# Window attention and feed-forward in one kernel: the first layer's first three steps split by head pair, weights joined into buffers of their own, the first loads on a second queue, and another order

## The chip, the core and the metric

The kernel runs on one core of a Trainium2 chip. The core has five engines that run side by side: TensorE (PE) for matmuls, VectorE (DVE), ScalarE (ACT), GpSimd (POOL), and SyncE (SP), which here only issues DMAs. Each engine works through its own instructions in order and waits at an instruction whose inputs are not there yet. PE writes to eight banks of PSUM; everything else lives in SBUF. The metric is the device time of one launch in microseconds, lower being better.

## What is computed

Eight batches of eight heads, 512 local and 32 global tokens, head size 64. A local query sees the 32 global keys and the local keys within 32 positions; a global query sees all keys. The 4352 result rows of 512 numbers then pass through a feed-forward layer of width 2048.

```python
s_g = scale * np.matmul(q_g, k_all.transpose(0, 1, 3, 2))
out_g = np.matmul(sm(s_g), v_all)
s_ll = np.where(np.abs(pos[:, None] - pos[None, :]) <= 32, scale * np.matmul(q_l, k_l.transpose(0, 1, 3, 2)), -1e9)
a_l = sm(np.concatenate([scale * np.matmul(q_l, k_g.transpose(0, 1, 3, 2)), s_ll], axis=-1))
out_l = np.matmul(a_l, v_all)
x = np.concatenate([out_g, out_l], axis=2).transpose(0, 2, 1, 3).reshape(B * S, H * D)
h = x @ w_in
g = h - np.tanh(h)
return g @ w_out
```

The two weight matrices arrive as 64-bit floats.

## The kernel before

**Precision.** Most operands are kept as a rounded high part and a low remainder, so one product is three passes on PE: high by high, low by high, high by low. The first two batches of attention ("plain", `Pair`) work on unsplit 32-bit data, two heads at a time; from the third batch on (`Head`) operands are split. Of the feed-forward layer, an engine other than PE makes each split: a cast (ACT or DVE) and a subtraction (mostly POOL).

**Weights.** There are 64 pieces of 128x256, in the order `w_in`, `w_in`, `w_out`, `w_out` for each of 16 hidden tiles f. For each piece `add_weights` issues a load into one of three buffers `wraw` (L364), then ACT rescales the upper words (L375), DVE shifts the lower ones (L379) and joins both in place (L383), ACT casts the high part (helper at L308) and POOL subtracts (L389). The buffer is free for the next load when the last of these has read it.

**Feed-forward layer.** A `Chunk` is the 512 local tokens of one batch, in 16 steps; a last chunk holds the 256 global tokens. A step's hidden part (L1090) is 12 matmuls of 128x512 into one bank: three passes over the four quarters of the 512 inputs. Then come tanh on ACT (L1098), the difference on DVE (L1101), the cast `ghi` and the remainder `glo` (L1107 on POOL). The step's output part (L1138) is 12 matmuls that add into four banks. x of a batch is complete when its last head pair's product (L602 in plain batches) has been cast into `x_hi` and `x_lo`.

**Overlap.** While batch b is in the feed-forward layer, the attention of batch b+1 runs between its steps. For a split head i: scores with the global queries (L779, L780), local scores (L831, L832) which read keys `kw` and queries `hi`/`hl` that DMAs have rearranged, softmax on DVE, ACT, DVE and POOL, then the product of head i-1 (L1008) which also carries the transposes of head i (L1010). So the last product of a batch waits for the scores of the next batch's first head, and a batch's feed-forward chunk cannot begin before it. I call the stretch where one chunk ends and the next begins a batch boundary; five of them (the ends of chunks 1 to 5, counted from 0) are followed by attention of a further batch.

**What sets the order.** Nothing is ordered by hand: every operation is added to `Order` with estimated durations, the keys that it reads and writes, and a due number; `Order.run` then plays the program through with these estimates and always takes the operation that can start first, the smaller due number deciding near ties. The due numbers and the penalties that choose between engines come from the table `CFG`. The order so found is emitted engine by engine. All DMAs are issued by SP in that order.

```python
                    key = (s, o.due, o.seq)
                    if best is None or s < best[0] + self.TOL and (
                            s < best[0] - self.TOL or (o.due, o.seq) < (best[1], best[2])):
                        best = (s, o.due, o.seq, o, e, d, used, t0)
```

## Time and profile before

| what | value |
|---|---|
| time, median of three runs | 1061.52 us (1059.08 to 1063.37) |
| time of the profiled execution | 1059.53 us |
| its span, first to last instruction | 1057.8 us |
| mean granted TensorE clock | 0.981 |
| moved by DMA | 91.69 MB, mean 87 GB/s |
| matmul records | 5656 |

The span is what the views of the trace cover; the 1.7 us beside it lie around it. "Busy" of PE counts overlapping matmuls once, and their ends are modelled, so the start of one to the start of the next is the better measure of a matmul's price.

### The profile page before, as it was taken

The page shows a single profiled execution, that of the slowest core. Times are in us where ns is not written, and L with a number is a line of the kernel's source. Part 1 is how long each engine was busy: PE and PEld are TensorE (multiplying, and loading weights), DVE is VectorE, ACT ScalarE, POOL GpSimd, SP SyncE. Part 2 cuts the span into 40 slices and gives each one's busy share as a digit, 9 for nine tenths or more (in the row PEclk, how much of TensorE's full clock was granted, in tenths as well). Part 3 has the DMA queues.
Part 4 walks back from the last instruction along what each step waited for, and adds up shares of the span by engine and source line. Part 5 has one row for each costly group of instructions (what it writes and reads, how often), then busy time and mean ns, then how long its engine had stood idle before and what let it go on. Part 6 is the DMA issues. An engine that isn't in the chain of part 4 may idle for free.

```text
span 1057.8 us, 19135 instructions
## 1 busy us (share of the span) xinstructions
PE 1009.3 (95%) x5656; PEld 837.6 (79%) x5656; DVE 661.7 (63%) x2084; ACT 608.4 (58%) x1684; POOL 625.9 (59%) x875
## 2 busy tenths in 40 slices
PE   6779999999996999999999999999999999999997
PEld 4557777788885888878888888888887888888896
DVE  7855666667664876687766786587757776322221
ACT  6856666656655765477657766577647765310121
POOL 5645556567664776677756776577666766522221
PEclk9979999999996999999999999999999999999999
DMA  8643444633235333454335432454335431000010
GB/s 209 166 124 106 128 113 126 143 78 82 57 77 127 79 78 69 83 137 87 73 64 137 91 85 59 95 130 86 80 60 133 91 70 42 33 8 1 1 40 20
DMA packets 253639, 91.69 MB, mean 87 GB/s; under 512 B 205408, under 2 KB 238944, under 8 KB 253536
## 3 DMA queue, kind: packets, MB, share of 16 engines
q1 hardware_dynamic: 253536, 90.48, 36.3%
q8 instruction: 45, 0.74, 0.3%
q14 instruction: 58, 0.48, 0.2%
HBM read 49.27 MB, written 8.91 MB: 55 GB/s over the span
## 4 chain that ended last, share of the span: by engine, by line
PE 88%; SPq 2%; DVE 2%; DMA 2%; issue 2%; ACT 2%; POOL 1%; POOLq 0%; ACTq 0%; DVEq 0%
PE bank L1090 35%; PE bank L1138 34%; PE bank L1008 5%; PE bank L1010 4%; PE bank L831 2%; PE bank L832 2%; PE bank L922 1%; PE bank L602 1%; PE bank L581 1%; PE bank L779 1%; SPq L640 1%; DMA hl<-hl 1%; PE bank L512 1%; DMA wraw<-in_moe_w_in_dram 1%; PE bank L780 1%
## 5 line engine op out<-in xcount | busy, mean ns | idle before, releaser
L1107 POOL TENSOR_TENSOR glo<-t,ghi 128x512 fp32r<-128x512 f32 x136 | 176.0, 1295 | 183.7 <-DVE ghi L308 80.7
L1101 DVE TENSOR_TENSOR t<-bank,t 128x512 f32<-128x512 f32 x136 | 93.8, 690 | 166.0 <-ACT t L1098 164.7
L1098 ACT ACTIVATE t<-bank 128x512 f32<-128x512 f32 x136 | 81.4, 598 | 189.4 <-PE bank L1090 172.3
L1138 PE MATMUL bank<-w_out_hi,ghi 128*128 128x512 f32 x544 | 153.9, 397 | 3.6 <-ACT ghi L308 3.6
L1138 PE MATMUL bank<-w_out_lo,ghi 128*128 128x512 f32 x544 | 154.4, 398 | 0.0
L1138 PE MATMUL bank<-w_out_hi,glo 128*128 128x512 f32 x544 | 153.4, 396 | 0.4 <-POOL glo L1107 0.4
L856 POOL TENSOR_SCALAR prob<-prob,st 128x224 f32<-128x224 f32 x240 | 108.2, 464 | 61.7 <-DVE st L851 39.6
L1090 PE MATMUL bank<-x_hi,w_in_hi 128*128 128x512 f32 x512 | 141.8, 399 | 0.4 <-ACT x_hi L308 0.4
L1090 PE MATMUL bank<-x_lo,w_in_hi 128*128 128x512 f32 x512 | 142.0, 400 | 0.0
L1090 PE MATMUL bank<-x_hi,w_in_lo 128*128 128x512 f32 x512 | 140.8, 397 | 0.0
L843 ACT ACTIVATE prob<-prob,st 128x224 f32<-128x224 f32 x240 | 113.4, 474 | 22.1 <-DVE st L836 20.7
L1138 PEld LDWEIGHTS bank<-w_out_hi,ghi 128*128 128x128 f32 x544 | 100.6, 188 | 25.1 <-ACT ghi L308 4.3
L836 DVE CUSTOM_DVE_ANT_0 prob<-bank,mask 128x224 f32<-128x224 f32 x240 | 83.4, 387 | 51.2 <-PE bank L832 41.1
L1138 PEld LDWEIGHTS bank<-w_out_lo,ghi 128*128 128x128 f32 x544 | 100.0, 189 | 19.4
L1138 PEld LDWEIGHTS bank<-w_out_hi,glo 128*128 128x128 f32 x544 | 99.2, 188 | 20.5 <-POOL glo L1107 0.8
L1090 PEld LDWEIGHTS bank<-x_hi,w_in_hi 128*128 128x128 f32 x512 | 94.6, 191 | 21.7 <-issue 1.2
L1090 PEld LDWEIGHTS bank<-x_lo,w_in_hi 128*128 128x128 f32 x512 | 92.2, 190 | 17.4 <-issue 0.6
L1090 PEld LDWEIGHTS bank<-x_hi,w_in_lo 128*128 128x128 f32 x512 | 92.1, 189 | 17.5
L1010 PE MATMUL bank<-idr,prob 128*128 128x128 f32 x376 | 99.4, 283 | 4.2 <-POOL prob L856 2.6
L1008 PE MATMUL bank<-thi,vv 128*128 128x160 f32 (+2 forms) x384 | 97.8, 296 | 0.0
L1043 POOL TENSOR_TENSOR x_lo<-wraw,x_hi 64x256 fp32r<-64x256 f32 x96 | 70.7, 736 | 39.6 <-ACT x_hi L308 26.9
L1008 PE MATMUL bank<-tlo,vv 128*64 128x160 f32 (+2 forms) x384 | 90.0, 235 | 0.0
(138 smaller groups left out, 1934.2 us busy)
## 6 DMA issues: line engine op xcount, KB each, us to landing
hl<-hl SPq DMA_DIRECT2D x72, 128.0 KB, 2.3
wraw<-in_moe_w_in_dram SPq DMA_DIRECT2D x32, 256.0 KB, 2.9
wraw<-in_moe_w_out_dram SPq DMA_DIRECT2D x32, 256.0 KB, 3.1
out_dram<-wraw SPq DMA_DIRECT2D x32, 256.0 KB, 2.3
kw<-hl SPq DMA_DIRECT2D x72, 96.0 KB, 2.2
vraw<-in_v_l_dram SPq DMA_DIRECT2D x48, 128.0 KB, 2.2
rawkq<-in_k_l_dram SPq DMA_DIRECT2D x96, 64.0 KB, 2.3
rawkq<-in_q_l_dram SPq DMA_DIRECT2D x96, 64.0 KB, 2.4
```

The source lines that it names most:

```text
L831: nc.tensor.matmul(t_[:, i, :KC], part_lo()[:, q], kw2()[:, t], start=True, stop=False)
L836: nc.vector.tensor_tensor_reduce(out=self.tile(t)[:, :KC], in0=getattr(self, f"s_{pair}")[:, i, :KC], in1=tile_mask[t], scale=-0.125, scal ...
L843: nc.scalar.activation(x, x, AF.Exp, bias=self.st[:, t:t + 1], scale=-1.0, accum_out=self.st[:, 4 + t:5 + t])
L856: nc.gpsimd.tensor_scalar(x, x, self.st[:, 8 + t:9 + t], 1.0, op0=ALU.mult, op1=ALU.mult)
L1008: nc.tensor.matmul(dst, l, r, start=i == 0, stop=i == len(mm) - 1, skip_group_check=True)
L1010: nc.tensor.transpose(*turns[i // each], idn)
L1043: eng[e].tensor_sub(places()[1], view(total, [(160, 2), (1, P)]), f32(places()[0]))
L1090: nc.tensor.matmul(self.h[s][:, j * n:(j + 1) * n], w[:, cc, f * P:(f + 1) * P], self.x()[xi][:, cc, :n], start=part == 0 and cc == 0 and ...
L1098: nc.scalar.activation(tt_[q], self.h[s], AF.Tanh)
L1101: nc.vector.tensor_sub(tt_[q], self.h.pop(s), tt_[q])
L1107: eng[e].tensor_sub(gg[q][1], tt_[q], f32(gg[q][0]))
L1138: nc.tensor.matmul(self.acc[tt], g[:, j * self.n + tt * P:j * self.n + (tt + 1) * P], low_out(f) if wi else w_out_hi[:, f], start=s == 0 a ...
```

## The change

Six things change together.

1. **Steps 0 to 2 of chunk 0 are split by head pair.** Instead of three passes over all four quarters of x, there are four operations of three matmuls (L1162), one for each quarter. A quarter of x comes from one head pair, so its three matmuls can run as soon as that pair's product is there. The bank of the hidden step is held from the first of them on.
2. **Weights are joined into other buffers.** There are four `wraw` buffers instead of three (the fourth shares its place with `qgt`, which is used later), and the join writes into one of two halves of `vraw` (`whole`). The load buffer is free after the join; the cast and the subtraction read the half.
3. **First loads on ACT.** The keys and queries of the first head pair are issued by ACT.
4. **Values are loaded for both heads of a pair in one operation**, which needs both heads' products of the pair before to be done, and the two heads of a pair share one pair of instructions for the inverse sums.
5. **Fewer memsets at the start.** `vraw` and `gt` are cleared later, the three banks not at all, of `first_v` only a 32x64 corner.
6. **The planner has other estimates** (semaphore delays, durations, a term for a change between matmul shapes) and nearly all numbers of `CFG` are new, so the order changes over the whole program.

```diff
-    SEM = {"T": 0.21, "A": 0.13, "D": 0.13, "P": 0.15, "S": 0.1}
+    SEM = {"T": 0.21, "A": 0.06, "D": 0.06, "P": 0.06, "S": 0.1}
+    FAR = {"A": 0.08, "D": 0.1}
+    HELD = {"T": 0.0, "A": 0.1, "D": 0.085, "P": 0.04, "S": 0.0}
+    TURN = 0.2
...
-    qgt = cp.tile([P, H, 2, G], F32R, name="qgt")
+    wraw.append(cp.tile([P, 256, 2], F32, name="wraw3", tag="qgt"))
...
+    whole = vraw.rearrange("p a t d -> p a (t d)")
...
-               ho=15.4658, hs=5.4507, lag=23.9151, last=0.0, newb=2, o_ld=77.6741, o_pv=13.7172, o_pvp=1.1836, o_s=-26.7655,
+               d_v=18.7031, d_w=40.8472, d_wl=13.7854, d_wn=3.035, d_xg=3.3383, d_y=0.5073, gfirst=0, ho=12.6631, hs=6.1049, lag=11.2597, last=0.0,
...
         def join(e, _):
-            v, up = box["v"].bitcast(I32), box["raw"][:, :, 1].bitcast(I32)
-            nc.vector.scalar_tensor_tensor(v, up, 3, v, op0=ALU.logical_shift_left, op1=ALU.bitwise_or)
+            v, up = [box["raw"][:, :, k].bitcast(I32) for k in range(2)]
+            box["v"] = whole[:, n % 2]
+            nc.vector.scalar_tensor_tensor(box["v"].bitcast(I32), up, 3, v, op0=ALU.logical_shift_left, op1=ALU.bitwise_or)
...
+        wj = ("wj", n % 2)
-            add(("D", 0.42), join, due, r=[key], w=[key], lock=True)
-        add(either(256, "w"), high, due, r=[key], w=[("w", kind, f, j, 0)])
-        add(subtract(256, "w"), rest, due, r=[key, ("w", kind, f, j, 0)], w=[("w", kind, f, j, 1)], res=spot)
+            add(("D", 0.42), join, due, r=[key], w=[wj], lock=True)
+        add(either(256, "w"), high, due, r=[wj], w=[("w", kind, f, j, 0)])
+        add(subtract(256, "w"), rest, due, r=[wj, ("w", kind, f, j, 0)], w=[("w", kind, f, j, 1)], res=spot)
...
-                add(("S", 1.2), load(a, (k_l, q_l)[a]), self.due(self.C["o_ld"] - 8), w=[self.key[a]], xfer=1.46)
+                add(("S" if self.j else "A", 1.1), load(a, (k_l, q_l)[a]), self.due(self.C["o_ld"] - 8) if self.j else -200 + a,
+                    w=[self.key[a]], xfer=1.46)
...
+            early = name.startswith("b0") and s < EARLY
+            for cc in range(NCC if early else 0):
+                r = [k + (xi,) for k in self.xkeys if k[2] // 2 == cc for xi in range(2)]
+                r += [("w", "i", s, cc // 2, wi) for wi in range(2)]
+                at = due if cc == NCC - 1 else base(2 * cc) + CFG["o_h0"] + CFG["hp"] * s
+                add(("T", 0.69), some(cc), at, r=r, w=[hk], res=[tk] if cc == 0 else (), alloc=[(hk, "h")] if cc == 0 else ())
-            for part in range(3):
+            for part in range(0 if early else 3):
```

Where instructions now stand is shown at three places. First, on PE near the end of the first batch's attention. Before, the hidden steps 0 and 1 (L1090) stand behind the last product (L602), four matmuls to a row:

```order
L602 MATMUL bank_105<-first_t_95,first_v 64x160
L602 MATMUL bank_105<-first_t_96,first_v 64x160
L1090 MATMUL bank_103<-x_hi_99,w_in_hi 128x512 x4
L1090 MATMUL bank_101<-x_hi_99,w_in_hi 128x512 x4
L1090 MATMUL bank_103<-x_lo_100,w_in_hi 128x512 x4
L1090 MATMUL bank_101<-x_lo_100,w_in_hi 128x512 x4
L1090 MATMUL bank_103<-x_hi_99,w_in_lo 128x512 x4
L1090 MATMUL bank_101<-x_hi_99,w_in_lo 128x512 x4
L1138 MATMUL bank_108<-w_out_hi,ghi_74 128x512
```

In the changed kernel, on PE while the third and fourth head pairs are still in their softmax (L1162 hidden, L649 product, L566 and L972 transposes, L617 scores):

```order
L1162 MATMUL bank_102<-x_hi_97,w_in_lo 128x512
L649 MATMUL bank_105<-first_t_93,first_v 64x160
...
L566 MATMUL bank_104<-idr,pg 96x64
L1162 MATMUL bank_99<-x_hi_97,w_in_hi 128x512
L1162 MATMUL bank_99<-x_lo_98,w_in_hi 128x512
L1162 MATMUL bank_99<-x_hi_97,w_in_lo 128x512
L972 MATMUL bank_106<-idr,prob_80 128x128 x4
L972 MATMUL bank_103<-idr,t_71 128x128 x4
L1162 MATMUL bank_102<-x_hi_97,w_in_hi 128x512
...
L617 MATMUL bank_100<-first_kw,first_q 128x224
```

Of the 24 matmuls of steps 0 and 1, 18 now stand ahead of the last product and six behind it; step 2 has its twelve behind the first eight output matmuls.

Second, on SP at the start of the program, before (`first_raw` are keys and queries of a pair, `first_v` its values):

```order
L420 DMA wraw_69<-in_q_g_dram 32x8x64
L364 DMA wraw_67<-in_moe_w_in_dram 128x2x256
L463 DMA first_raw<-in_k_l_dram 128x4x64 x2
L463 DMA first_raw<-in_q_l_dram 128x4x64 x2
L364 DMA wraw_68<-in_moe_w_in_dram 128x2x256
L364 DMA wraw_69<-in_moe_w_out_dram 128x512
L958 DMA first_v<-in_v_l_dram 128x3x64
```

In the changed kernel the same place on SP; the first pair's keys and queries are ACT's first four DMAs, and the `first_raw` rows here are the second pair's:

```order
L433 DMA wraw_69<-in_q_g_dram 32x8x64
L375 DMA wraw_78<-in_moe_w_in_dram 128x2x256
L375 DMA wraw_67<-in_moe_w_in_dram 128x2x256
L588 DMA first_v<-in_v_l_dram 128x7x64
...
L476 DMA first_raw<-in_k_l_dram 128x4x64 x2
L375 DMA wraw_68<-in_moe_w_out_dram 128x512
L375 DMA wraw_69<-in_moe_w_out_dram 128x512
L476 DMA first_raw<-in_q_l_dram 128x4x64 x2
```

The second pair's keys were SP's 16th row, behind four weight loads and both heads' values; now they are the 9th, behind two weight loads.

Third, on PE at the end of chunk 1, where batch 3's first head begins. Before, all output matmuls (L1138) come first, then the global scores (L779), the local scores (L831) and at once the product with transposes (L1008, L1010):

```order
L1138 MATMUL bank_105<-w_out_lo_1587,ghi_72 128x512
L1138 MATMUL bank_105<-w_out_hi,glo_73 128x512
L779 MATMUL bank_101<-kw,qgt 128x384
L780 MATMUL bank_102<-kw,qgt 128x224
L831 MATMUL bank_103<-kw,hl 128x224
...
L832 MATMUL bank_101<-kw,hi_1866 128x224
L1008 MATMUL bank_102<-thi,vv 128x160
L1008 MATMUL bank_102<-tlo,vv 64x160
L1010 MATMUL bank_103<-idr,prob_81 128x128
```

In the changed kernel, on PE at the same boundary, from the end of the scores on (L880 scores, L1199 output, L1053 and L1055 product and transposes):

```order
L1199 MATMUL bank_104<-w_out_hi,glo_73 128x512
L879 MATMUL bank_100<-kw,hl 128x224
...
L880 MATMUL bank_99<-kw,hi_1831 128x224
L1199 MATMUL bank_103<-w_out_hi,ghi_74 128x512
...
L1199 MATMUL bank_104<-w_out_hi,glo_75 128x512
L1053 MATMUL bank_101<-thi,vv 128x160
L1053 MATMUL bank_101<-tlo,vv 64x160
L1055 MATMUL bank_100<-idr,prob_79 128x128
```

Between the last global scores of batch 2 (L827 of its last head) and the first of batch 3 there are now 18 groups of four 128x512 matmuls and two products with transposes; 12 output matmuls then stand between the global and the local scores, 12 between these and the product, and six behind each of the two products. The four later boundaries of this kind have the same order.

More of the change, by code (lines that the diff above doesn't have):

```diff
@@ L1110, in add_hidden, with some, fn @@
             fs = range(s * self.per, (s + 1) * self.per)
-            for part in range(3):
+            def some(cc):
+                def fn(e, tags):
+                    if cc == 0:
+                        self.h[s] = bank([P, 512], tags[hk])
+                    for part, (wi, xi) in enumerate(((0, 0), (0, 1), (1, 0))):
+                        nc.tensor.matmul(self.h[s], (w_in_hi, w_in_lo)[wi][:, cc, s * P:(s + 1) * P], self.x()[xi][:, cc],
+                                         start=cc == 0 and part == 0, stop=cc == NCC - 1 and part == 2)
+                return fn
+            early = name.startswith("b0") and s < EARLY
[5 more added lines that the diff above has]
+            for part in range(0 if early else 3):
                 wi, xi = ((0, 0), (0, 1), (1, 0))[part]
```

205 lines of the change are left out of this document (121 added, 84 removed).

## The prediction

> **What bounds the kernel now.** I read the page's first part, then its chain of work that ended last, then windows by stage.
>
> ```profile
> PE 1009.3 (95%) x5656; PEld 837.6 (79%) x5656; DVE 661.7 (63%) x2084; ACT 608.4 (58%) x1684; POOL 625.9 (59%) x875
> PE 88%; SPq 2%; DVE 2%; DMA 2%; issue 2%; ACT 2%; POOL 1%; POOLq 0%; ACTq 0%; DVEq 0%
> 0.00:75.36 75.36, 56.09 (x364) 39.70 (x364) 57.16 (x242) 50.43 (x154) 39.94 (x78) 0.89 0.67 173
> 80.00:300.00 220.00, 216.20 (x1225) 172.49 (x1224) 143.65 (x474) 141.70 (x398) 135.07 (x184) 1.00 0.41 103
> 310.00:345.00 35.00, 24.84 (x121) 20.46 (x120) 16.27 (x57) 20.17 (x56) 16.60 (x25) 0.76 0.55 125
> 430.00:465.00 35.00, 32.84 (x190) 27.75 (x189) 23.06 (x70) 22.24 (x60) 21.26 (x29) 1.00 0.50 120
> 795.00:830.00 35.00, 33.00 (x201) 28.14 (x199) 26.84 (x89) 26.01 (x73) 24.53 (x35) 1.00 0.53 126
> ```
>
> The last five rows are windows: their bounds and length, then busy time (records) of PE, PEld, DVE, ACT and POOL, the granted clock, the share of the DMA engines and GB/s. PE is the bound. The change removes hardly any matmul, so it can gain only where PE idles or runs at a lowered clock. From 80 to 300 PE idles 3.8 us of 220 at full clock: no order gains much there. Two stretches are left. In the **opening**, to the first tanh at 75.36, PE idles 19.3 us at a clock of 0.89. At the **first batch boundary**, 310 to 345, it idles 10.16 us at 0.76. Later boundaries are nearly full: 2.16 us idle in 430 to 465, 2.00 in 795 to 830, both at 1.00.
>
> **Term A, the opening.** How it ends shows in the timelines of PE and ACT (start, duration, engine, line, operation, tiles, count, and in brackets the idle time before and its releaser):
>
> ```profile
> 63.08 4.18 PE L602 MATMUL bank<-first_t,first_v 128*64 128x160 f32 x30 [1.06 <-DMA first_v<-in_v_l_dram]
> 67.19 1.35 PE L1090 MATMUL bank<-x_hi,w_in_hi 128*128 128x512 f32 x3
> 70.25 1.98 PE L1090 MATMUL bank<-x_lo,w_in_hi 128*128 128x512 f32 x8
> 72.06 1.97 PE L1090 MATMUL bank<-x_hi,w_in_lo 128*128 128x512 f32 x8
> 74.36 0.43 ACT L375 ACTIVATE wraw<-wraw 128x256 f32<-128x256 f32 x1 [3.02 <-DMA wraw<-in_moe_w_in_dram]
> 75.36 0.58 ACT L1098 ACTIVATE t<-bank 128x512 f32<-128x512 f32 x1
> 77.64 1.56 PE L1138 MATMUL bank<-w_out_hi,ghi 128*128 128x512 f32 x4 [3.60 <-ACT ghi L308]
> ```
>
> Between the last product's end at 67.19 and the tanh at 75.36 lie 8.17 us: 24 hidden matmuls, and on ACT a rescaling of weights, ahead of the tanh in its queue, that waited 3.02 for its load. Then PE idles 3.60 until `ghi`.
>
> *A1, behind the last product.* The new order puts 18 of those 24 matmuls ahead of the last product. Eight take 72.06 − 70.25 = 1.81, 0.226 each, so six take 1.36. With a cast `x_hi` (0.364, row below) and some 0.8 for waits between engines, about what the same hand-overs took here beside their work, I estimate 2.5 in place of 8.17: **−5.7**. The 18 moved matmuls fit into PE's 19.3 us of idle time. If ACT's weight wait stayed ahead of the tanh, only the matmuls would go, 18 × 0.226 = 4.1.
>
> *A2, ahead of it.* ACT's groups up to 80 us (count, busy time, mean ns, idle before):
>
> ```profile
> L375 ACT ACTIVATE wraw<-wraw 128x256 f32<-128x256 f32 x27 | 11.9, 441 | 16.3 <-DMA wraw<-in_moe_w_in_dram 10.8 <-DMA wraw<-in_moe_w_out_dram 4.4 <-DMA first_v<-in_v_l_dram 0.4
> L308 ACT CAST w_in_hi<-wraw 128x256 fp32r<-128x256 f32 x14 | 5.8, 421 | 1.6 <-DVE wraw L383 1.4
> L308 ACT CAST x_hi<-bank 128x256 fp32r<-128x256 f32 x7 | 2.5, 364 | 0.1
> L308 ACT COPY first_q<-bank 128x512 f32<-128x512 f32 x3 | 1.7, 570 | 0.0
> L308 ACT COPY first_t<-bank 128x512 f32<-128x512 f32 x13 | 7.4, 577 | 2.5 <-PE bank L922 2.5
> L308 ACT COPY first_t<-bank 128x128 f32<-128x128 f32 x1 | 0.3, 283 | 0.0
> L308 ACT COPY first_t<-bank 96x32 f32<-96x32 f32 x1 | 0.2, 209 | 0.0
> 2.15 1.02 SPq L463 DMA_DIRECT2D first_raw<-in_k_l_dram  x2
> ```
>
> ACT waited 10.8 + 4.4 = 15.2 us for weight loads, with everything behind it queued; 3.0 of it is the wait in A1, 12.2 lies earlier. The loads wait for buffers. What holds one:
>
> ```profile
> wraw<-in_moe_w_in_dram SPq DMA_DIRECT2D x32, 256.0 KB, 2.9
> L379 DVE TENSOR_SCALAR wraw<-wraw 128x256 int32<-128x256 int32 x27 | 9.1, 346 | 7.2 <-DMA wraw<-in_moe_w_in_dram 6.7 <-DMA wraw<-in_moe_w_out_dram 0.3
> L383 DVE SCALAR_TENSOR_TENSOR wraw<-wraw 128x256 int32<-128x256 int32 x27 | 11.1, 421 | 1.3 <-ACT wraw L375 0.5
> L389 POOL TENSOR_TENSOR w_in_lo<-wraw,w_in_hi 128x256 fp32r<-128x256 f32 x14 | 10.3, 741 | 20.8 <-ACT w_in_hi L308 20.8
> ```
>
> Before: 2.9 + 0.44 + 0.35 + 0.42 + 0.42 + 0.74 = 5.27 us, over three buffers 1.76 a piece. Now the hold ends with the join, 4.11 us, over four 1.03. The new order rescales 23 pieces ahead of the first tanh where before it was 27: 23 × 1.03 = 24 us in place of 27 × 1.76 = 47. As the loop halves, I take half of the 12.2: **−6**. The bounds are 0 (the 16 DMA engines, at a share of 0.67 here, cannot bring the loads sooner) and −12.2.
>
> Does ACT get more work? Counted in the new order ahead of the first tanh: four rescalings, four casts, five `x_hi` and three `first_q` fewer (−1.76 − 1.68 − 1.82 − 1.71), two more large `first_t` copies (+1.15), seven more pairs of small ones (7 × 0.49 = +3.44), three other copies (at most 0.57 each, +1.7), four DMA issues (two took 1.02, so +2.04): +1.4 at most, which the 24.9 us that ACT idles hide; without that cover they cost 1.4. The moved loads start the first pair at most 2.1 us (those two pairs of issues on SP) sooner, and the second pair's keys, now behind two weight loads, wait for fewer buffers; both lie within A2's bounds. DVE only loses work here: pieces, halved inverse instructions, memsets and small copies, against five `x_hi` casts and three `first_q` copies more; its 57.16 busy of 75.36 hides the rest.
>
> The Trainium skill, page "DMA: Bandwidth & Descriptors", section "Issuing engines are not separate DMA queues", says that DMAs started by different engines run on the same 16 and that a second issuer saves only issue time. By it the move to ACT is worth no more than the issues above, and the sum stands.
>
> *A3, an added wait.* A pair's values now are one operation of four DMAs, which needs both products of the pair before.
>
> ```profile
> 67.41 1.16 SPq L958 DMA_DIRECT2D first_v<-in_v_l_dram  x2
> 68.62 0.59 SPq L969 DMA_DIRECT2D first_v<-in_v_g_dram  x1
> ```
>
> One head's issues took 1.75; the first head's can no longer start while the second's product runs. Queued behind on SP are weight loads, and PE's products wait for the values: it waited 1.06 at 63.08. Three pairs reload in the opening, so the bounds are 0 (transposes and softmax cover it) and 3 × 1.75 = 5.3. I take one, **+1.7**, as there was one such wait. In the second batch the reloads lie beside a PE that is full from 80 on, and cost nothing; uncovered, four pairs would cost 7.0.
>
> A = −5.7 − 6 + 1.7 = **−10.0**.
>
> **Term B, the first boundary.** PE's timeline: first prices and the last global scores of the old batch, then the boundary:
>
> ```profile
> 301.02 0.34 PE L779 MATMUL bank<-kw,qgt 128*128 128x384 f32 x1
> ...
> 302.23 1.10 PE L1138 MATMUL bank<-w_out_hi,ghi 128*128 128x512 f32 x4
> 303.16 1.09 PE L1138 MATMUL bank<-w_out_lo,ghi 128*128 128x512 f32 x4
> 304.09 0.23 PE L1008 MATMUL bank<-thi,vv 128*128 128x160 f32 x1
> ...
> 305.03 1.18 PE L1138 MATMUL bank<-w_out_hi,glo 128*128 128x512 f32 x4
> ...
> 323.28 0.34 PE L831 MATMUL bank<-kw,hl 128*128 128x224 f32 x1 [2.97 <-DMA hl<-hl]
> ...
> 324.41 0.36 PE L1008 MATMUL bank<-thi,vv 128*128 128x160 f32 x1
> ...
> 327.48 0.48 PE L1010 MATMUL bank<-idr,prob 128*128 128x128 f32 x1 [2.58 <-POOL prob L856]
> ...
> 334.79 0.52 PE L831 MATMUL bank<-kw,hl 128*128 128x224 f32 x1 [2.78 <-DMA hl<-hl]
> ```
>
> Four 512-column matmuls cost 0.93, a product with transposes 0.94, a head's local scores 324.41 − 323.28 = 1.13. Idle is 10.16, and a clock of 0.76 over 35 us means 16.8 us at half; less the waits of 2.58 and 2.78 in it, 11.4 us of work ran at half and lost 5.7. In all 15.9 against a full PE.
>
> The new order spreads output matmuls over the waits. What must happen in between took, by the trace: from the last global scores to the next head's local scores 323.28 − 301.02 = 22.26; there now stand 21 groups and two products, 19.5 + 1.9 = 21.4, so 0.9 is missing. Scores to transposes took 4.2; now 1.13 and three groups, 3.9: 0.3 missing. Scores to the next head's scores took 11.5, or 8.9 without the 2.58 that the late transposes added; now 1.13 + 6 × 0.93 + 2 × 0.94 = 8.6: 0.3 to 2.9, taken in the middle, 1.6. Idle left is 2.8, near the later boundaries' 2.0 to 2.2, where the clock stayed at 1.00. So B = −(10.16 − 2.8) − 5.7 = **−13.1**, bounds 0 and −15.9.
>
> The Trainium skill, page "TensorE: Matmul & The Clock Gate", section "HAM oscillation — how this bites in real kernels", says that idle gaps above some 3.4 us halve the rate. The trace differs: waits of 2.97 and 2.58 led to it. By the page no gap up to the 2.9 above would cost any clock; by the trace a gap of 2.9 could keep half of the 5.7 lost, and the sum would be 4 higher with that gap (1.3 of idle, 2.9 of clock).
>
> The other four boundaries have the same new order and idle about 2 now: 0, bounds ±2 each by what they idle now. The steady part, PE full: 0, bounds −3.8 by its idle time and as much above for changes between kinds of matmul. The tail: as before.
>
> **Sum.** 1059.53 (profiled execution) − 10.0 − 13.1 = 1036.4. The median of the runs is 2.0 above that execution, so I predict a median of **1038**; the rivals get the same 2.0.
>
> **Rivals.**
> - *The boundary keeps its stall.* If the new batch's loads are late because SP issues them behind others, more matmuls ahead don't help. Against it: the waits were filled exactly where they stood. Only A: 1049.5 + 2 = 1051. Chance 0.13.
> - *The weight loads stay late*, since the DMA engines, at 0.67, share them with all that was moved forward; A comes to nothing. For it: no window shown here moves more than 177 GB/s (row under the next rival). Only B: 1046.4 + 2 = 1048. Chance 0.12.
> - *The clock in the opening rises too*, as the 18 matmuls fill gaps.
>
> ```profile
> 50.00:60.00 10.00, 8.08 (x45) 5.82 (x45) 7.56 (x36) 8.09 (x28) 7.68 (x15) 0.66 0.33 98
> 60.00:70.00 10.00, 8.06 (x43) 6.06 (x44) 6.11 (x18) 4.96 (x14) 4.28 (x7) 0.66 0.64 177
> ```
>
>   At 0.66, 6.8 us of each ten ran at half; PE was busy 81% of it, so 11.0 us of work lost 5.5. Against it: the matmuls moved are only 4 us of PE. 1030.9 + 2 = 1033. Chance 0.12.
> - *Slower: the boundary's stall spreads to all.* All five boundaries are now built alike, with the cover that I reckon 2.8 short at the first. If the real chain of loads, scores and softmax is longer, each idles as the first did and falls to half clock. Then four more pay 15.9 − 2.2 = 13.7: 1059.5 − 10.0 + 54.8 + 2 = 1106. It decides from where idle time per boundary passes a point between 2.2 (clock 1.00) and 10.2 (0.76). For it: the matmuls between two heads' scores are few. Against it: the chain had the same parts at 795 to 830 and lost 2.0. Chance 0.07.
> - *Nothing moves*, gains returned in the second batch, which inherits weights that are late: 1061.5. Chance 0.05.
>
> **How the numbers follow.** The forecast has 0.51, its own range 1031 to 1047 (A from −5 to −14, B from −10 to −16). The range for 8 in 10 is 1022 to 1056: downward A1, A2 and B at their far bounds, A3 at 0, with the opening's clock (1059.5 − 5.7 − 12.2 − 15.9 − 5.5 + 2 = 1022), upward the two rivals with one term, with that term at half. Under 0.5%, some 5 us, no measurement of this kernel can tell from no change. Faster: 0.51 + 0.13 + 0.12 + 0.12, less 0.02 for their upper ends, 0.86. Within: 0.05 + 0.01 = 0.06. Slower: 0.07 + 0.01 = 0.08.
>
> **What would show it.** A: the first output matmul at 66 to 69 in place of 77.64; ACT's waits for weight loads near 6 in place of 15.2; no weight wait of 3 ahead of the first tanh. A3: PE's waits for `first_v` near 2.8 in place of 1.06. B: the window of the first boundary at a clock of 1.00 with some 3 us idle. Wrong would be: a clock under 0.9 there, idle of over 3 at later boundaries, or a steady part that idles over 7 of 220.

## The result and the profile after

| | before | changed |
|---|---|---|
| median of the runs | 1061.78 us (4 runs, 1059.08 to 1063.37) | 1033.42 us (4 runs, 1032.14 to 1034.15) |
| ratio to before | | 0.9734, 95% interval 0.9711 to 0.9757 |
| span of the profiled execution | 1057.8 us | 1030.3 us |

2.7% faster, 4.6 us below the prediction of 1038 and inside its range. The page of the changed kernel, its engines' busy times:

```profile
PE 1002.9 (97%) x5656; PEld 829.0 (80%) x5656; DVE 612.1 (59%) x1913; ACT 670.6 (65%) x1824; POOL 619.4 (60%) x871
```

The same matmuls, in a shorter span. Windows of the changed kernel (columns as in the prediction): the opening up to the first tanh, a stretch of 220 us behind it, the first boundary, and the second:

```profile
0.00:62.80 62.80, 49.00 (x362) 35.34 (x363) 49.61 (x201) 47.13 (x157) 35.75 (x73) 0.99 0.77 185
65.00:285.00 220.00, 219.76 (x1249) 176.25 (x1250) 151.07 (x474) 156.99 (x443) 142.45 (x198) 1.00 0.47 113
285.00:335.00 50.00, 48.05 (x276) 40.24 (x275) 33.29 (x103) 37.39 (x104) 33.25 (x49) 1.00 0.47 104
400.00:450.00 50.00, 48.82 (x284) 40.76 (x283) 32.46 (x98) 36.94 (x100) 32.76 (x48) 1.00 0.48 108
```

The first boundary idles 1.95 us at a clock of 1.00, where before it idled 10.16 at 0.76, and is now like the second. The opening still idles 13.8 us, but at 0.99. Its end in the timelines of PE and ACT, and ACT's waits for weight loads up to 76 us (what waited for what, then total, times, longest):

```profile
56.49 2.24 PE L649 MATMUL bank<-first_t,first_v 128*64 128x160 f32 x32
61.08 0.77 PE L1162 MATMUL bank<-x_hi,w_in_hi 128*128 128x512 f32 x1 [2.36 <-DVE x_hi L319]
62.80 0.60 ACT L1144 ACTIVATE t<-bank 128x512 f32<-128x512 f32 x1
65.18 1.20 PE L1199 MATMUL bank<-w_out_hi,ghi 128*128 128x512 f32 x4 [1.19 <-ACT ghi L319]
ACT wraw L386 <- DMA wraw<-in_moe_w_out_dram: 5.9, 8, 2.9
ACT wraw L386 <- DMA wraw<-in_moe_w_in_dram: 2.5, 3, 1.8
```

The first output matmul starts at 65.18 in place of 77.64, 12.46 us sooner: the last product ends at 58.73 in place of 67.19 (8.46), and from there to the tanh it takes 4.07 in place of 8.17 (4.10). ACT waits 8.4 us for weight loads, before 15.2.

To see where the gain lies and stays, both kernels can be compared at equal work. PE's records, in order, hold 2.05 million columns of moving data in both; the table gives when a kernel had started on a given share of them (worked out from all 5656 records):

| columns started, thousands | before, us | changed, us | difference |
|---|---|---|---|
| 24 | 32.98 | 33.27 | +0.3 |
| 36 | 43.63 | 42.51 | −1.1 |
| 60 | 71.61 | 57.66 | −14.0 |
| 84 (opening over) | 89.78 | 74.98 | −14.8 |
| 288 | 194.01 | 180.73 | −13.3 |
| 528 (ahead of the first boundary) | 312.36 | 295.07 | −17.3 |
| 576 (behind it) | 351.74 | 320.52 | −31.2 |
| 1200 | 651.63 | 621.93 | −29.7 |
| 2016 | 1035.35 | 1007.91 | −27.4 |

The opening gained 14.8, nearly all of it (12.9) between 43 and 72 us of the time before, the first boundary 13.9, the second batch 2.5; 3.8 were given back in small pieces over the rest. So two places made the gain, as forecast. What remained open was what in them did it.

### The profile page after: what moved, and what is told of

It reads as the page before. It is cut to its first block, busy times and chain, and to the rows that moved or that the text cites. A ratio compares the mean times of both kernels' runs of the same rounds, so it can differ in the third digit from the quotient of the medians.

```text
span 1030.3 us, 18920 instructions
## 1 busy us (share of the span) xinstructions
PE 1002.9 (97%) x5656; PEld 829.0 (80%) x5656; DVE 612.1 (59%) x1913; ACT 670.6 (65%) x1824; POOL 619.4 (60%) x871
## 4 chain that ended last, share of the span: by engine, by line
PE 85%; DVE 6%; ACT 3%; DMA 2%; issue 2%; SPq 1%; POOL 0%; DVEq 0%; ACTq 0%
PE bank L1199 34%; PE bank L1136 31%; PE bank L1053 5%; PE bank L1055 4%; PE bank L879 2%; PE bank L880 2%; PE bank L649 1%; PE bank L617 1%; PE bank L972 1%; DVE pg L839 1%; DMA out_dram<-wraw 1%; ACT prob L891 1%; PE bank L1162 1%; PE bank L827 1%; PE bank L526 1%
## 5 line engine op out<-in xcount | busy, mean ns | idle before, releaser
L1199 PE MATMUL bank<-w_out_hi,ghi 128*128 128x512 f32 x544 | 155.6, 399 | 1.2 <-ACT ghi L319 1.2
L1199 PE MATMUL bank<-w_out_hi,glo 128*128 128x512 f32 x544 | 154.8, 398 | 0.0
L1199 PE MATMUL bank<-w_out_lo,ghi 128*128 128x512 f32 x544 | 154.1, 397 | 0.0
L1136 PE MATMUL bank<-x_hi,w_in_hi 128*128 128x512 f32 x500 | 138.5, 399 | 0.0
L904 POOL TENSOR_SCALAR prob<-prob,stats 128x224 f32<-128x224 f32 x240 | 105.9, 455 | 53.2 <-ACT ghi L319 18.7
L1136 PE MATMUL bank<-x_lo,w_in_hi 128*128 128x512 f32 x500 | 136.8, 395 | 0.0
L1136 PE MATMUL bank<-x_hi,w_in_lo 128*128 128x512 f32 x500 | 136.3, 394 | 0.0
L319 ACT CAST ghi<-t 128x512 fp32r<-128x512 f32 x136 | 84.2, 619 | 63.8 <-PE bank L1199 51.9
L891 ACT ACTIVATE prob<-prob,stats 128x224 f32<-128x224 f32 x240 | 113.3, 474 | 19.0 <-DVE stats L884 18.2
L1199 PEld LDWEIGHTS bank<-w_out_hi,glo 128*128 128x128 f32 x544 | 100.9, 189 | 24.9 <-POOL glo L1153 2.0
L1199 PEld LDWEIGHTS bank<-w_out_lo,ghi 128*128 128x128 f32 x544 | 101.2, 188 | 21.9
L1199 PEld LDWEIGHTS bank<-w_out_hi,ghi 128*128 128x128 f32 x544 | 99.0, 189 | 22.0 <-ACT ghi L319 2.1
L1136 PEld LDWEIGHTS bank<-x_hi,w_in_hi 128*128 128x128 f32 x500 | 89.8, 189 | 17.5 <-issue 0.7
L1055 PE MATMUL bank<-idr,prob 128*128 128x128 f32 x376 | 98.3, 280 | 1.9 <-DVE tlo L989 1.0
L1053 PE MATMUL bank<-thi,vv 128*128 128x160 f32 (+2 forms) x384 | 97.0, 294 | 0.0
L319 ACT COPY wraw<-bank 64x288 f32<-64x288 f32 (+1 forms) x125 | 54.9, 439 | 60.0 <-PE bank L1053 27.1
```

Source lines behind the costliest of these rows:

```text
L319: (nc.scalar.copy if e == "A" else nc.vector.tensor_copy)(dst, src)
L891: nc.scalar.activation(x, x, AF.Exp, bias=self.st[:, t:t + 1], scale=-1.0, accum_out=self.st[:, 4 + t:5 + t])
L904: nc.gpsimd.tensor_scalar(x, x, self.st[:, 8 + t:9 + t], 1.0, op0=ALU.mult, op1=ALU.mult)
L1053: nc.tensor.matmul(dst, l, r, start=i == 0, stop=i == len(mm) - 1, skip_group_check=True)
L1055: nc.tensor.transpose(*turns[i // each], idn)
L1136: nc.tensor.matmul(self.h[s][:, j * n:(j + 1) * n], w[:, cc, f * P:(f + 1) * P], self.x()[xi][:, cc, :n], start=part == 0 and cc == 0 and ...
```

## Experiments

In most of these kernels the order was first worked out as in the kernel they start from; then only the named operations got another place on their engine, and nothing else was planned anew. So an effect belongs to the edit and not to a fresh order. Line numbers in their rows are higher by the lines added. The edits are given as short diffs in which `rank` is an operation's place in the order. The other parts of the change (the split of the third step, the memsets, the joint load of values and the shared inverse sums) were not tried apart.

### The split of the first steps

```diff
+    for s in range(2):
+        for cc in range(3):
+            rank[by["E", s, cc].seq] = rank[by["E", s, 3].seq] - 0.1 * (3 - cc)
```

("E", s, cc) are the three matmuls of step s on quarter cc of x.

> The changed kernel with its order kept on every engine, except that the 18 split hidden matmuls of steps 0 and 1 stand again behind the last product. The first output matmul starts at 65.2 us in the changed kernel and at 77.6 in the one before. Theory (the split takes matmuls out of the end of the opening): 18 x 0.226 = 4.1 us come back, first output at 69 to 70. Theory with clock (the early matmuls also kept the clock up between 42 and 60 us): half clock comes back in that stretch, another 2 to 5 us, first output at 71 to 75 and a granted clock of about 0.7 from 45 to 60. Rival (weight loads set the end, the matmuls only filled gaps): first output before 67.

And with the places kept busy:

```diff
-                    for part, (wi, xi) in enumerate(((0, 0), (0, 1), (1, 0))):
+                    fill = s < 2 and cc < 3
+                    for c in range(0 if s < 2 and cc == 3 else cc, cc + 1):
+                        for part, (wi, xi) in enumerate(((0, 0), (0, 1), (1, 0))):
...
+                                             start=fill or c == 0 and part == 0, stop=fill or c == NCC - 1 and part == 2)
```

> As the run before it, but where the 18 matmuls stood early the same 18 are still issued, with their result overwritten by the later ones: PE is as busy as in the changed kernel and does 18 matmuls more. Theory: first output at 69 to 70, clock near 0.99 up to 60 us. If the clock is part of the gain, this kernel is faster than the run before it by 2 to 5 us although it does more work; if the clock has no part, both have the same time, or this one is slower.

Measured: 1032.30 us (ratio 0.9722, 0.9688 to 0.9755) and 1033.14 (0.9734, 0.9700 to 0.9767), both the time of the changed kernel. First the split moved back, then the one with the places filled: the windows from 40 to 60 us, and the first output matmul.

```profile
40.00:50.00 10.00, 7.72 (x55) 5.22 (x55) 9.55 (x43) 9.17 (x33) 6.68 (x11) 0.77 0.73 167
50.00:60.00 10.00, 9.38 (x87) 7.99 (x84) 7.88 (x25) 7.93 (x26) 6.67 (x13) 0.88 0.64 178
...
58.20 0.50 PE L1204 MATMUL bank<-x_hi,w_in_hi 128*128 128x512 f32 x1
65.16 1.19 PE L1241 MATMUL bank<-w_out_hi,ghi 128*128 128x512 f32 x4 [1.19 <-ACT ghi L361]
```

```profile
40.00:50.00 10.00, 8.85 (x63) 5.84 (x63) 9.49 (x42) 9.42 (x34) 6.54 (x11) 1.00 0.59 154
50.00:60.00 10.00, 9.88 (x98) 8.05 (x95) 7.91 (x26) 7.56 (x26) 7.23 (x13) 1.00 0.72 188
...
65.35 1.19 PE L1239 MATMUL bank<-w_out_hi,ghi 128*128 128x512 f32 x4 [1.19 <-ACT ghi L357]
```

Two theories fall here. The split is worth nothing: with 24 matmuls behind the last product instead of six, the first output matmul starts at 65.16, not at 69. PE begins them at 58.20 without a wait; in the changed kernel the six wait until 61.08 for `x_hi`, which DVE casts behind pieces of weights, and then run at half clock, some 0.43 us from one to the next in place of 0.23. So both end at some 63.98. And the clock between 40 and 60 us is worth nothing either: without the early matmuls it falls to 0.77 and 0.88, with the filling it stays at 1.00, and the end is the same. The rival that the expectation named, that something else sets the end, is right: on ACT the first tanh stands behind weight pieces in both kernels (62.80 in the changed one, 62.53 here). PE is close behind it, though. The second tanh, ahead of the `ghi` that PE waits for, was released by PE after 0.33 us of idle time in the changed kernel and 0.59 here.

### The first pair's loads

```diff
-                        eng[e].dma_start(first_raw[self.set][:, a, :, h],
+                        nc.sync.dma_start(first_raw[self.set][:, a, :, h],
```

> The changed kernel with its order kept, but the four DMAs of the first head pair's keys and queries issued by SP behind its first two loads, as before, instead of by ACT. Theory (they only save issue time): the first transposes start 1 to 2 us later than 4.97, first output matmul 0 to 2 us later than 65.2. Rival (the second queue lets the loads run side by side, worth more): over 3 us.

Measured: 1035.68 us (0.9745, 0.9716 to 0.9773). PE's first transposes, its wait for `x_hi` and its first output matmul:

```profile
6.17 1.09 PE L535 MATMUL bank<-idr,first_raw 128*128 128x128 f32 x4 [6.17 <-DMA first_raw<-in_k_l_dram]
...
61.71 0.47 PE L1204 MATMUL bank<-x_hi,w_in_hi 128*128 128x512 f32 x1 [2.35 <-DVE x_hi L361]
...
65.36 1.19 PE L1241 MATMUL bank<-w_out_hi,ghi 128*128 128x512 f32 x4 [1.87 <-ACT ghi L361]
```

The start is 1.20 us later (4.97 in the changed kernel), as issue time alone would have it, and 0.2 of it is left at the first output matmul. The whole is 2 us slower, less than the intervals resolve. The wait for `x_hi` is as long as in the changed kernel (2.35 and 2.36), but here the six matmuls behind it run at full clock, the granted clock of the whole execution being 1.000; PE is done with them at 63.49 and then waits 1.87 for `ghi`. So the half clock of those six did not set the first output matmul either.

### The weight buffers

In place in three buffers, as before, under the new order; then all three parts undone together. Of a buffer's two numbers the first, used in planning, keeps the order, and the second is the buffer that is really used:

```diff
-            box["v"] = whole[:, n % 2]
-            nc.vector.scalar_tensor_tensor(box["v"].bitcast(I32), up, 3, v, op0=ALU.logical_shift_left, op1=ALU.bitwise_or)
+            nc.vector.scalar_tensor_tensor(v, up, 3, v, op0=ALU.logical_shift_left, op1=ALU.bitwise_or)
...
-        return ("wraw", wslot[i] % (2 if i else 4))
+        return ("wraw", wslot[i] % (2 if i else 4), wslot[i] % (2 if i else 3))
```

> The changed kernel with its order kept, but the weights joined in place again in three load buffers, which are held until the cast and the subtraction have read them. Theory (the buffer loop made the loads late): ACT's waits for weight loads up to 76 us rise from 8.4 to about 15, first output 4 to 8 us later, at 69 to 73. Rival (the loads are limited by the DMA engines, or ACT's waits lie beside other work): first output within 1 us of 65.2.

> The split back behind the last product, the weights in place in three buffers, and the first pair's loads on SP, all together, the rest of the order kept. Theory (these three parts are the gain of the opening, 12.5 us to the first output matmul): first output at 76 to 79. Rival (the new order of all the rest is most of it): first output at 66 to 72. The steady part after 80 us keeps its time in both.

Measured: 1150.24 us (1.0833, 1.0796 to 1.0869) and 1149.52 (1.0828, 1.0781 to 1.0875). The first is 117 us slower than the changed kernel, and the other two parts add nothing to it. Neither theory nor rival held: the first output matmul starts at 106.51 and 105.54, far behind every forecast, and the steady part lost time too. SP's waits of the first kernel from 60 to 300 us, and a window of it:

```profile
SPq L433 <- POOL w_in_lo L458: 80.4, 22, 8.3
SPq L433 <- POOL w_out_lo L458: 75.3, 21, 8.5
```

```profile
50.00:100.00 50.00, 33.33 (x184) 22.95 (x181) 19.69 (x78) 20.09 (x67) 14.66 (x26) 0.67 0.33 86
```

SP stands at 43 weight loads for POOL's subtraction, 156 us in all, and POOL works in an order made for loads that don't wait for it. All engines wait for one another: no engine is busy for more than 67% of this window. This does not say that the buffers are worth 117 us; it says that this order cannot be run without them. Two more runs bound what they are worth. The fourth buffer alone:

> The changed kernel with its order kept and the weights joined into the other buffer, but with three load buffers instead of four. Theory (release at the join is what the new order needs, the fourth buffer is a little more): 23 pieces x (4.11/3 - 4.11/4 = 0.34) = 8 us more in the loop at worst, of which some is hidden: first output at 66 to 73, the whole 1 to 10 us slower than the changed kernel. Rival (the count is what matters, as in the run with in-place joining): over 30 us slower.

Measured: 1073.58 us (1.0114, 1.0087 to 1.0140), 40 us slower than the changed kernel, so the rival; the first output matmul starts at 79.98. Released at the join but with three, SP still waits (waits up to 130 us, this kernel and then the changed one):

```profile
SPq L433 <- DVE vraw L453: 45.1, 23, 5.9
```

```profile
SPq L375 <- DVE vraw L395: 39.0, 24, 3.9
```

These waits for the join differ by 6 us only, while by then the kernel is some 21 us behind the changed one at equal work, and 42 at 223 us. So the loss is more than SP's waiting; what stands behind each late piece was not followed. And the other way round, the buffers put into the kernel before:

```diff
-            nc.vector.scalar_tensor_tensor(v, up, 3, v, op0=ALU.logical_shift_left, op1=ALU.bitwise_or)
+            box["v"] = whole[:, n % 2]
+            nc.vector.scalar_tensor_tensor(box["v"].bitcast(I32), up, 3, v, op0=ALU.logical_shift_left, op1=ALU.bitwise_or)
...
-        return ("wraw", wslot[i] % (2 if i else 3))
+        return ("wraw", wslot[i] % (2 if i else 3), wslot[i] % (2 if i else 3 if wslot[0] > 48 else 4))
```

> The kernel before with its order kept on every engine; only the weights are joined into the two halves of another buffer and the first 47 loads use four load buffers instead of three. Theory (the buffers by themselves bring the loads sooner): ACT's waits for weight loads up to 76 us fall from 15.2 to 8 or less, first output matmul at 70 to 74 instead of 77.6, the whole 3 to 8 us faster. Rival (the buffers are only a condition, the gain of the opening is the order that uses them): first output at 76 or later, the whole within 2 us.

In this kernel the values of the first split head are overwritten by weights before they are read, so that head's part of the output comes from other data; no instruction is left out.

Measured: 1060.50 us (0.9994, 0.9974 to 1.0014): no gain. First the kernel before, then this one: SP's waits up to 76 us; for this one also ACT's waits for weight loads and the first output matmul.

```profile
SPq L364 <- POOL w_out_lo L389: 10.1, 7, 3.4
SPq L364 <- POOL w_in_lo L389: 8.2, 6, 4.2
SPq L958 <- PE bank L602: 2.5, 3, 1.5
```

```profile
SPq L1025 <- PE bank L669: 14.3, 5, 6.1
SPq L427 <- DVE vraw L447: 3.1, 5, 1.4
...
SPq L427 <- DVE wraw L442: 2.0, 3, 1.2
...
ACT wraw L438 <- DMA wraw<-in_moe_w_in_dram: 8.9, 9, 2.7
ACT wraw L438 <- DMA wraw<-in_moe_w_out_dram: 1.7, 4, 0.7
...
75.30 2.01 PE L1205 MATMUL bank<-w_out_hi,ghi 128*128 128x512 f32 x4 [3.31 <-ACT ghi L371]
```

The waits of SP for buffers fall from 18.3 us to 5.1, as they should. But SP then stands in the same queue for PE's products, 14.3 us in place of 2.5: the values of a later head (L1025) may only be loaded when the products that use the buffer have read the earlier ones, and the weight loads stand behind. ACT still waits 10.6 us for loads, and the first output matmul comes 2.3 us sooner, between what theory and rival gave; the whole is unchanged, as the rival said. One wait took the place of another, on the same queue. The sum of SP's waits is no measure of late loads by itself: in the changed kernel SP waits 18.3 us for weight buffers up to 76 us, too, by its rows for `vraw` and `wraw`.

How fast the pieces pass shows on ACT. Counted in the traces, these are the rescalings of the 23rd and of the 27th piece in the kernel before, and of the 23rd in the changed one, the last ahead of each kernel's first tanh being the 27th and the 23rd:

```profile
66.28 0.44 ACT L375 ACTIVATE wraw<-wraw 128x256 f32<-128x256 f32 x1
...
75.03 0.44 ACT L375 ACTIVATE wraw<-wraw 128x256 f32<-128x256 f32 x1 [0.24 <-DMA wraw<-in_moe_w_out_dram]
```

```profile
62.04 0.45 ACT L386 ACTIVATE wraw<-wraw 128x256 f32<-128x256 f32 x1 [0.26 <-ACT w_out_hi L319]
```

The first tanh comes at 75.36 and at 62.80, so a piece takes 2.8 us before and 2.7 in the changed kernel: nearly the same pace. The 23rd piece is 4.2 us sooner, and the 8.75 us from the 23rd to the 27th fall away, because the new order puts four pieces fewer ahead of the first tanh. This is a count and not an experiment: no run moved these four alone.

### The boundary

Three kernels on the order of PE. First the changed kernel with all 36 last output matmuls moved ahead of the new batch's first scores:

```diff
+    late = [by["O", "b1", s, i] for s in (13, 14, 15) for i in range(4) if ("O", "b1", s, i) in by]
+    for n, o in enumerate(late):
+        rank[o.seq] = rank[by["G", 24].seq] - 0.9 + 0.05 * n
```

> The changed kernel with its order kept, except at the first boundary: the output matmuls of steps 13 to 15 of chunk 1 all stand ahead of the new batch's first global scores, as before. Theory (the order of matmuls is the gain of the boundary): waits come back ahead of the first product and of the second local scores, 6 to 9 us idle and a granted clock under 0.9 in the stretch from 285 to 335, the whole 8 to 14 us slower than the changed kernel. Rival (the new batch's loads and splits simply come earlier now, and the place of the output matmuls matters little): under 4 us.

Measured: 1042.42 us (0.9812, 0.9785 to 0.9838), 9.0 slower. Its window and PE's longest wait in it:

```profile
285.00:335.00 50.00, 42.52 (x225) 34.52 (x223) 27.21 (x81) 29.99 (x84) 27.44 (x39) 0.93 0.39 88
PE bank L1241 <- POOL glo L1195: 2.6, 1, 2.6
```

The stall comes back in part: 5.5 us more idle, the clock at 0.93, not under 0.9. With 27 groups of four feed-forward matmuls left in both kernels, the places of the 36 matmuls are worth 9.0 us, of the 13.9 that the boundary gained. Then the same places given to the output matmuls in the kernel before:

```diff
+    behind(("S", 24, 1), *[("O", "b1", 14, i) for i in range(3)])
+    behind(("P", 23, 0), ("O", "b1", 15, 0), ("O", "b1", 15, 1))
+    behind(("P", 23, 1), ("O", "b1", 15, 2), ("O", "b1", 15, 3))
```

> The kernel before with its order kept, except at the first boundary, where the output matmuls of steps 13 to 15 are put between scores and products just as in the changed kernel. Theory (the order on PE alone is the gain): 9 to 14 us faster than the kernel before. Rival (the keys arrive at 319.8 whatever PE does, so that matmuls put behind them only move the wait ahead of them): within 3 us, with a wait of 6 us or more ahead of the first global scores.

Measured: 1063.75 us (1.0016, 0.9993 to 1.0038): nothing gained. PE's longest wait from 300 to 350 us:

```profile
PE bank L826 <- DMA kw<-hl: 7.0, 1, 7.0
```

And the same wait in PE's timeline of the kernel before:

```profile
319.79 0.42 PE L779 MATMUL bank<-kw,qgt 128*128 128x384 f32 x1 [0.86 <-DMA kw<-hl]
```

The wait moved ahead of the first scores, 7.0 us in place of 0.86, as the rival said: whatever stands behind the new batch's scores is missing ahead of them. So in this kernel the places of these 36 matmuls decide nothing; it has too few matmuls left when the old batch's last global scores are done. From there the chain over the new batch's keys (buffer `kw` free, loads, splits, rearranging DMAs) to its first head's local scores takes 22.26 us before. Here are the last DMA of that chain in the kernel before, then the changed kernel's last global scores, the same DMA, and the local scores:

```profile
320.82 0.49 SPq L749 DMA_DIRECT2D hl<-hl  x1
```

```profile
273.49 0.34 PE L827 MATMUL bank<-kw,qgt 128*128 128x384 f32 x1
...
291.46 0.49 SPq L797 DMA_DIRECT2D hl<-hl  x1
...
295.54 0.27 PE L879 MATMUL bank<-kw,hl 128*128 128x224 f32 x1
```

295.54 − 273.49 = 22.05 us, without a wait in it on PE, so this is PE's own work: 21 groups at 0.93 and two products at 0.94 are 21.4. The chain itself was a little shorter: its last DMA was issued 17.97 us behind the last global scores, before 19.80. Counting in both orders the groups of four feed-forward matmuls that the chunk has left behind the last global scores gives, for the five boundaries: before 16, 27, 26, 26, 26; changed 27, 28, 28, 28, 28 (the later four have 19 groups ahead of the new scores, the first 18). The one stalled boundary was the one with 16. Only 3.83 us of its waits (0.86 and 2.97) were on this chain; the other long ones (2.58 and 2.78) stood behind the first local scores. To test the count, the changed kernel's PE got the order of the kernel before for 41 operations, so that 16 are left:

```diff
+    by = {o.name: o for o in ops if o.name}
+    at = sorted(rank[by[k].seq] for k in WINDOW)
+    for k, v in zip(WINDOW, at):
+        rank[by[k].seq] = v
```

> The changed kernel with its order kept, except that on PE the 41 operations from the last head's local scores of batch 2 to the second head's local scores of batch 3 stand in the order of the kernel before: 16 groups of four feed-forward matmuls are left behind the last global scores instead of 27. Theory (what decides is how much of the chunk is left there, since the chain from the last global scores to the next head's local scores takes about 22 us): 8 to 11 us idle in the stretch from 285 to 335, clock under 0.9, the whole 10 to 16 us slower than the changed kernel. Rival (the new batch's loads and splits come earlier for another reason): under 5 us.

Measured: 1053.89 us (0.9930, 0.9905 to 0.9956), 20.5 slower than the changed kernel:

```profile
285.00:335.00 50.00, 34.74 (x164) 28.21 (x163) 22.28 (x67) 24.80 (x66) 20.54 (x29) 0.83 0.35 77
...
296.38 2.00 PE L1181 MATMUL bank<-x_hi,w_in_hi 128*128 128x512 f32 x4 [3.56 <-DVE tlo L1034]
...
310.61 0.34 PE L872 MATMUL bank<-kw,qgt 128*128 128x384 f32 x1
...
318.90 0.47 PE L1100 MATMUL bank<-idr,prob 128*128 128x128 f32 x1 [5.26 <-POOL prob L949]
```

A stall is back, larger than it was: 13.3 us more idle, clock 0.83. But it isn't the one that the theory named. The new batch's global scores start at 310.61 without a wait, the local ones right behind them, so here the chain over the keys did not stall PE; it was shorter, its last DMA issued 15.81 us behind the last global scores. PE waits 3.56 us for DVE ahead of these scores, and 5.26 behind them for the new head's softmax, where this order leaves no feed-forward matmul to fill in. As this order also has all output matmuls ahead of the scores, 9.0 of the 20.5 us go by the first of these runs with the places, and some 11.5 are left for the smaller count and for an order on the other engines that doesn't fit it; these two were not separated. So the three runs show that PE's order makes the boundary: the right places without the count gain nothing, the count without the places keeps some 5 of the 13.9. That the 22 us chain alone decides is not shown.

Last, the price of the lowered clock alone, in the kernel before:

```diff
+                for _ in range({24: 13, 25: 12}.get(self.i, 0) if pair == 0 else 0):
+                    nc.tensor.matmul(banks[tags[s]], w_in_hi[:, 0, :P], w_out_hi[:, 0], start=True, stop=True)
```

(and 11 such matmuls ahead of the first product).

> The kernel before with 36 matmuls whose results are overwritten, put into PE's three long waits of the first boundary (13 ahead of the first local scores, 11 ahead of the first product, 12 ahead of the next local scores). Nothing that is waited for changes. Theory (the half clock from 324 to 341 came from these gaps and cost 5.7 us): the clock stays at 1.00, the kernel is 4 to 6 us faster than before although it does more. Rival (the clock, or its cost, is not tied to the gaps): no faster, or slower by what the fill delays.

Measured: 1058.97 us (0.9987, 0.9967 to 1.0006). The window of the boundary and two rows of PE's timeline; below them the product's row of the kernel before:

```profile
310.00:345.00 35.00, 30.44 (x157) 23.72 (x157) 18.35 (x61) 20.58 (x57) 18.41 (x27) 1.00 0.57 131
...
334.30 0.34 PE L871 MATMUL bank<-kw,hl 128*128 128x224 f32 x1 [0.92 <-DMA hl<-hl]
...
339.74 0.34 PE L1050 MATMUL bank<-thi,vv 128*128 128x160 f32 x1 [0.23 <-DVE st L829]
```

```profile
342.67 0.23 PE L1008 MATMUL bank<-thi,vv 128*128 128x160 f32 x1
```

The clock stays at 1.00, but the second head's scores still come at 334.30 (334.79 before): up to there a faster PE only waits longer. The clock counts almost only behind the last wait, where the next stretch of four hidden groups takes 5.4 us (334.30 to 339.74) and took 7.9 before (334.79 to 342.67). That is about 2.4 us, 2.9 with the 0.5 ahead of it, not 5.7. The whole moved by 1.4, inside its interval, which reaches to 3.5.

### A further step

> The changed kernel with two places moved: on DVE the last head pair's cast and subtraction of x (whose result PE waited 2.36 us for at 61 us) stand ahead of three pieces of weights, and at each of the five boundaries the second of the last step's four output operations stands behind the second product instead of ahead of it (PE waited 1.5 us ahead of the next scores at the first). Theory: 1 to 2 us at the opening and 1 to 2 at the boundaries, 1 to 4 us faster than the changed kernel. Rival (the waits come back elsewhere): within 1 us.

```diff
+    for n, k in enumerate((("XH", 3, 0), ("XL", 3, 0), ("XH", 3, 1), ("XL", 3, 1))):
+        rank[by[k].seq] = rank[by["PP", 3, 1].seq] + 0.1 * (n + 1)
+    for b in range(1, 6):
+        rank[by["O", f"b{b}", 15, 1].seq] = rank[by["P", 8 * b + 15, 1].seq] + 0.1
```

Measured: 1037.85 us (0.9779, 0.9754 to 0.9804), 4.4 slower than the changed kernel. DVE, ACT and PE at the end of the opening, and a window behind it:

```profile
58.05 0.42 DVE L705 TENSOR_TENSOR x_lo<-bank,x_hi 128x256 fp32r<-128x256 f32 x1 [1.55 <-ACT x_hi L362]
63.65 0.43 ACT L429 ACTIVATE wraw<-wraw 128x256 f32<-128x256 f32 x1 [1.96 <-DMA wraw<-in_moe_w_out_dram]
64.28 0.59 ACT L1187 ACTIVATE t<-bank 128x512 f32<-128x512 f32 x1
66.30 2.07 PE L1242 MATMUL bank<-w_out_hi,ghi 128*128 128x512 f32 x4 [5.26 <-ACT ghi L362]
...
65.00:75.00 10.00, 8.70 (x25) 6.90 (x26) 4.20 (x9) 4.70 (x12) 4.71 (x6) 0.66 0.39 114
```

PE waits only 0.62 us for `x_hi`, and the tanh still comes 1.5 us later. DVE now waits 1.55 us at the head of its queue, the joins behind it come later, ACT's casts wait for them, a load waits for its buffer, and the tanh stands behind all that in ACT's queue. PE then waits 5.26 us. So what sets the end of the opening is the queue of weight pieces on DVE and ACT ahead of the tanh; this is also why the split is worth nothing. In the profiled execution (the slowest of five, 7.7 us above the changed kernel's) the loss at equal work is 1.1 at the first output matmul and 3.9 at 72 us: behind the wait of 5.26 the clock is halved from 65.7 to 72.5, where PE has work without a pause, and that alone costs some 2.8. Another 3.6 come between 384 and 773 us, where later boundaries lie.

## Why the prediction was right, and where it was not

- **The bound.** PE is the bound, and only idle time and clock in the two named places could be gained: right. The two gave 14.8 and 13.9 of the 27.5 us by which the span fell.
- **A1, the split (−5.7).** The stretch from the last product to the tanh did become 4.10 us shorter, but not through the split, which was shown to be worth nothing (in steps 0 and 1; step 2 was left split). The step that failed is "18 of those 24 matmuls ahead of the last product": it priced matmuls on an engine that wasn't the bound there. The prediction had the true one in hand, the rescaling of weights that stood ahead of the tanh in ACT's queue, and used it only for a lower bound. The 3.02 us wait went; a wait of 1.84 ahead of the same tanh remains.
- **A2, the buffers (−6).** ACT's waits fell by 6.8, to 8.4, near the half that was taken, and the last product comes 8.46 us sooner. But the loop's price of a piece, 1.76 to 1.03, was the wrong account. A piece took 2.8 us before and 2.7 in the changed kernel, and the larger part of the 12.6 us lies in the four pieces that no longer stand ahead of the first tanh; the prediction counted these (27 to 23), but multiplied them with its loop. The buffers alone shortened the opening by 2.3 and the kernel by nothing, since SP's next wait, for values, took over. The gain belongs to the buffers and the new order together, and neither half has it alone: the old order with new buffers gives 1060.5, the new order with fewer or held buffers 1074 and 1150. Which part of the new order lets SP get on was not separated; the four pieces, the joint load of a pair's values and the earlier place of keys among the loads are the candidates.
- **A3, the joint values (+1.7).** No wait of PE for `first_v` is left up to 80 us in the changed kernel. The term is 0, its lower bound.
- **Issue on ACT.** Within the 2.1 us reckoned: 1.2 us at the start, 0.2 at the end of the opening.
- **B, the boundary (−13.1).** Right in mechanism and nearly in size, 13.9: 1.95 us idle in 50 where 2.8 was forecast. Three corrections. The sentence that the order "spreads output matmuls over the waits" is half of it: undoing it costs 9.0, but in the kernel before the same spreading gains nothing. The other half is its count of cover, 21 groups and two products against a chain of 22.26; that the chain is what stalls where the cover is short was seen in the kernel before and in the run with other places, and not in the run made to test it. The term's split into 7.4 of idle time and 5.7 of clock was off: the clock by itself is worth 2.4 to 2.9, since up to its last wait PE at full clock only waits longer. And of the waits that were said to lead to the half clock, that of 2.58 ended at 327.5, behind its start at 324.0.
- **The other boundaries and the steady part (0, bounds given).** The second batch gained 2.5, the 700 us behind the boundary gave back 3.8, spread over all of it; neither was traced to a cause. Together 1.3 on the wrong side.
- **The rivals.** "The clock in the opening rises too" gave 1033, and the clock did rise to 0.99. Its mechanism is not borne out: with the clock back at 0.77 and 0.88 between 40 and 60 us the time is the same. The half clock of the kernel before from 61.2 to 68.0, under its last product, was not tried by itself. Agreement in a number is no evidence for its mechanism. "The stall spreads to all" did not happen; PE's idle time at the later ones is 0.6 to 1.8 us in 50. The run with PE's old order shows that a stall of that price, 20.5 us at one boundary, was within reach. "The boundary keeps its stall" and "the weight loads stay late" did not happen.

So the sum was right, 23.1 forecast of 27.5 measured, while A was put together from the wrong pieces, and its nearness, 10.0 to 14.8, is in part luck. The shares of A that the runs leave are: split 0, issue on ACT 0.2, buffers alone 2.3, and the rest only from buffers and order together.

## What to carry to other kernels

Before pricing work that moves off an engine, look at who is late next there: at the end of this opening PE could take 18 more matmuls for nothing, because the tanh stood behind weight pieces in another engine's queue. Count also how many such pieces the order puts ahead of the first result. A buffer that is freed sooner only helps if the queue that loads it isn't held by something else in order, so count the waits of that queue by what they wait for. And for a hand-over between two batches, count how much independent work is left when the chain begins (the boundary with 16 groups stalled, those with 26 to 28 did not), and where it stands: with 16 groups the other places gained nothing, but with 27 the old places cost 9.0 us.

## What the runs showed of the hardware

The lowered clock came in pieces that are near multiples of 3.4 us in the trace's clock records: before, from 16.8 to 20.2, 51.0 to 57.8, 61.2 to 68.0, 78.3 to 81.7, 324.0 to 341.1 and at the end; in the changed kernel only from 61.0 to 64.4 and at the end. A wait's length alone does not tell whether it follows. A wait of 2.36 us was followed by it (at 61 us of the changed kernel), while the same wait of 2.35 at 61.71 us, with the first pair's loads on SP, was not, and one of 1.53 us ahead of the local scores at 306 was not. The Trainium skill, page "TensorE: Matmul & The Clock Gate", section "HAM oscillation — how this bites in real kernels", puts the limit at gaps of some 3.4 us; here 2.36 was enough once, and ahead of 324.0 no wait was longer than 2.97. What else decides is not shown.

The price depends on what PE has to do meanwhile. 17 us of it at the boundary cost only 2.4 to 2.9, since at full clock PE came to its last wait there only 0.5 us sooner (334.30 in place of 334.79); 6.8 us of it behind the opening of the further step, where PE had work without a pause, cost some 2.8.
